# Expert tiles 18 to 24 of a mixture-of-experts stage put into conditional blocks

## The chip, the cores and the metric

The kernel runs on one core of a Trainium2 chip. A core has a matrix engine (TensorE, PE in the profile; its weight loads are shown apart as PEld), a vector engine (VectorE, DVE), a scalar engine (ScalarE, ACT), a general engine (GpSimd, POOL) and a queue engine that issues transfers (SyncE, SP). Each engine takes its own instructions in order and waits on semaphores for the others; 16 DMA engines move data between memory and the on-chip buffers. The metric is the device time of one execution in microseconds (us), as the median of the runs.

## The reference

Sliding-window attention over 8 batches, 8 heads, 576 positions and 64 columns per head is followed by a layer of eight experts over the 4608 resulting tokens of 512 columns. Each token goes to the one expert with the largest router logit:

```
logits = x @ w_gate                       # 4608 x 8
expert_idx = np.argmax(logits, axis=1)
gate_w = probs[np.arange(N), expert_idx]
for e in range(E):                        # 8 experts, rows sorted by expert
    h = np.maximum(x_sorted[lo:hi] @ w1[e], 0.0)     # 512 -> 1024
    y_sorted[lo:hi] = h @ w2[e]                      # 1024 -> 512
return gate_w[:, None] * y_sorted[inv_perm]
```

The inputs come from a fixed seed, so how many tokens each expert gets is the same in every run.

## The kernel before, in words

There are three stages. The first, attention (lines 76 to 282), also computes the router's logits and writes the tokens x to memory (x_dram). The second, routing (lines 285 to 400), gives every token a slot. Slots are grouped in tiles of 256 (TB), and a tile belongs to one expert. Eight experts can leave at most seven extra partly filled tiles, so the kernel provides 4608 / 256 = 18 tiles (NCUT) and 7 more: 25 tiles in all (NTILE), enough for any routing. cum (line 359) holds the running count of tiles that the experts need; its last column is the number of tiles that hold any token. perm_i holds the token of every slot, and a slot without a token points past the end.

The third stage (lines 403 to 470) works through all 25 tiles, one after the other, whether a token lies in them or not. For a tile, fetch reads the tile's expert number from tile_e into a register of SP (line 413), loads w1 and w2 of that expert (2 MB each, lines 415 and 417, from SP) and gathers the 256 token rows in two indirect transfers from POOL (xg, line 421). The rest is the work on the tile: TensorE transposes the rows (tp, line 437), DVE and ACT copy them to the buffer xgT (line 438), TensorE computes hp = w1 x (line 445: 32 instructions, which the profile records as 64 matmuls), DVE and ACT apply the maximum with zero (lines 450 and 452), TensorE computes yp in two halves (line 456: 16 instructions, recorded as 32 matmuls), DVE scales the first half and ACT the second (lines 465 and 463), and POOL scatters each half to the output rows (line 467), leaving out the slots without a token.

w1 and w2 have two buffers each, xg has three of each half, y has four. fetch(i + 1) stands ahead of the work on tile i in the program, and a scheduler then orders the instructions of each engine. Each engine keeps its own order, so SP loads the weights as soon as a buffer is free (w1 of tile i + 2 when hp of tile i is done, w2 of tile i + 2 when yp of tile i is done), and POOL gathers the rows of later tiles between the scatters of earlier ones.

Of the kernel before, what the change touches and what calls it, by code (L numbers as in the profile page):

```python
# [10 lines left out]
F32 = mybir.dt.float32  # L11
I32 = mybir.dt.int32
# [6 lines left out]
WINDOW = 64  # L19
# [3 lines left out]
def _ins(ap: bass.AP, axis: int, n: int) -> bass.AP:  # L23
    """The view of ap that repeats it n times along a new dimension at axis."""
    dims = [list(d) for d in ap.ap]
    dims.insert(axis, [0, n])
    return bass.AP(tensor=ap.tensor, offset=ap.offset, ap=dims)
# [7 lines left out]
def kernel(  # L35
# [10 lines left out]
    nc = tc.nc  # L46
    P = nc.NUM_PARTITIONS
    B, H, S, D = q.shape
    NT, DM = out.shape
    E = moe_w_gate.shape[1]  # L50
    FF = moe_w1.shape[2]
    scale = 1.0 / math.sqrt(D)

    NG = H // 2              # head pairs: one pair fills the 128 partitions
    NB = S // WINDOW         # query blocks of one window; each sees itself and the block before
    GB = 3                   # query blocks handled together
    KB = (S + P - 1) // P    # row tiles of 128, the last one half full
    NV = NB // 2             # whole ones
    SM = NV * P
    BG = 2                   # batches that together fill whole token blocks  # L60
    NTB = BG * S // P        # token blocks in such a group
    NJ = NT // P             # token blocks in all
    FT = FF // P
    TB = 256                 # slots of one expert tile
    C = TB // P
    NTILE = (NT + TB - 1) // TB + E - 1   # enough for any routing
    NS = NTILE * C
    NCUT = (NT + TB - 1) // TB
# [5 lines left out]

    # x in token order, and after it one row of zeros for the slots without a token
    x_dram = dram.tile([NT + 1, DM], F32, name="x_dram")
# [6 lines left out]
    gate_s = consts.tile([P, NS], F32, name="gate_s")  # L83
    tile_e = consts.tile([P, NTILE], I32, name="tile_e")
    zrow = consts.tile([1, DM], F32, name="zrow")
    nc.vector.memset(zrow[:], 0.0)

# [1 line left out]
    with (  # L89
# [11 lines left out]
    ):  # L101
        # additive masks over [(head, query), key]: slot 0 for the first block, whose
        # keys are blocks 0 and 1; the others for the keys of the block before and its own
        mask = att_c.tile([P, 1 + GB, P], F32, name="mask")
        nc.gpsimd.memset(mask[:], 0.0)
        for h in range(2):
# [5 lines left out]
            for m in range(1, 1 + GB):  # L112
# [7 lines left out]
                )  # L120
        # q transposed, each head of the pair in its own columns and zeros beside it
        NQ = 2
# [18 lines left out]
        def load_v(b):  # L141
            va = vp.tile([P, NV, H, D], F32, name="va")
            vb = vp.tile([P, NV, H, D], F32, name="vb")
            for j in range(NV):
                nc.sync.dma_start(out=va[:, j], in_=v[b, :, j * P : (j + 1) * P, :].rearrange("h p d -> p h d"))
            nc.sync.dma_start(out=vb[D:P, NV - 1], in_=v[b, :, SM:S, :].rearrange("h p d -> p h d"))
            # the same keys half a tile later
            nc.gpsimd.tensor_copy(
                out=vb[0:D].rearrange("p j h d -> p (j h d)"), in_=va[D:P].rearrange("p j h d -> p (j h d)")
            )  # L150
            nc.gpsimd.tensor_copy(
                out=vb[D:P, 0 : NV - 1].rearrange("p j h d -> p (j h d)"),
                in_=va[0:D, 1:NV].rearrange("p j h d -> p (j h d)"),
            )
            return va, vb
# [127 lines left out]

# [1 line left out]
    with (  # L285
# [11 lines left out]
        iotas = []  # L297
        e_m = iota([P, E], [[1, E]], base=-E)                    # e - E
        lane = iota([P, P], [[1, P]])
        hi_id = iota([P, NS], [[1, NS]])  # L300
        tile_id = iota([P, NTILE], [[1, NTILE]])
        cuts = iota([P, NCUT], [[TB, NCUT]])
        tok_m = iota([P, NJ], [[P, NJ]], base=-NT, cm=1)         # token - NT, never 0
        before = rt.tile([P, P], F32, name="before")             # [p', p] = p' < p
        ones = rt.tile([P, P], F32, name="ones")
# [4 lines left out]
        )  # L310
        keep = rt.tile([P, E, NJ], F32, name="keep")             # 0 where a scan starts again
        nc.gpsimd.memset(keep[:], 1.0)
        nc.gpsimd.memset(keep[:, :, 0:1], 0.0)

        V = nc.vector
        by_tok = lambda t: t[:].rearrange("p e j -> p j e")
        per_e = lambda t, n: _inner(t[:], n)

        # the first expert of the largest logit, and its probability
        mx = rt.tile([P, NJ], F32, name="r_mx")  # L320
# [14 lines left out]

        # rank of a token among those of its expert: lower partitions of its column, columns before
        ohf = oh[:].rearrange("p e j -> p (e j)")
# [12 lines left out]

        # tiles of each expert, up to and with it, and the slot where it starts
        over = rt.tile([P, E, NCUT], F32, name="over")
# [15 lines left out]
        V.tensor_scalar_min(te[:], te[:], float(E - 1))  # L368
        V.tensor_copy(out=tile_e[:], in_=te[:])

        V.tensor_tensor(out=rank[:], in0=rank[:], in1=per_e(start, NJ), op=ALU.add)
# [11 lines left out]

        # the other way round: token and gate of every slot [slot % P, slot // P]
        lo = rt.tile([P, NJ, P], F32, name="lo")
# [15 lines left out]

# [1 line left out]
    w1v = moe_w1.rearrange("e (g p) f -> p e g f", p=P)  # L403
    w2v = moe_w2.rearrange("e (t p) d -> p e t d", p=P)
    with (
# [21 lines left out]

        fetched = {0: fetch(0)}
        for i in range(NTILE):
            if i + 1 < NTILE:  # L430
                fetched[i + 1] = fetch(i + 1)
            w1, w2, xg = fetched.pop(i)
            xgT = mp.tile([P, NG, TB], F32, name="xgT")
# [19 lines left out]
            for c in range(C):  # L453
                yp = ps_y.tile([P, DM], F32, name="yp")
                for f in range(FT):
                    nc.tensor.matmul(  # L456
                        yp[:], lhsT=hT[:, f, c * P : (c + 1) * P], rhs=w2[:, 0, f, :],
                        start=(f == 0), stop=(f == FT - 1),
                    )
                s = i * C + c  # L460
                y = mp.tile([P, DM], F32, name="y", bufs=4)
                if c % 2:
                    nc.scalar.activation(out=y[:], in_=yp[:], func=AF.Copy, scale=gate_s[:, s : s + 1])  # L463
                else:
                    nc.vector.tensor_scalar_mul(y[:], yp[:], gate_s[:, s : s + 1])  # L465
                # slots without a token point past the end and are left out
                nc.gpsimd.indirect_dma_start(  # L467
                    out=out[:, :], out_offset=bass.IndirectOffsetOnAxis(ap=perm_i[:, s : s + 1], axis=0),
                    in_=y[:], in_offset=None, bounds_check=NT - 1, oob_is_err=False,
                )  # L470


# [26 lines left out]
```

## Time and profile before

| | us |
|---|---|
| median of three runs | 1118.84 |
| lowest and highest run | 1118.69, 1123.08 |
| span of the profiled execution, first to last instruction | 1121.2 |
| TensorE busy in it | 1031.5 (92%) |
| DVE, ACT, POOL busy in it | 350.9, 277.1, 211.8 |

The profile describes one execution; its span is 2.4 us longer than the median of the runs. The attention stage lasts to about 335 us, routing to about 370 us, and the 25 tiles take the rest.

### The profile page before, as it was taken

Reading aid. Unit: us, or ns where it says so; the run is one execution under the profiler, and the core shown is the slowest. Engines: PE = TensorE matmul, PEld = TensorE weight load, DVE = VectorE, ACT = ScalarE, POOL = GpSimd, SP = SyncE. Lnnn points to the kernel's source line nnn. Section 1 sums busy time; section 2 is a strip of 40 time slices with the busy share of each in tenths; the row PEclk is TensorE's granted clock in tenths of the full one; section 3 lists DMA queues with packets and bytes.
Section 4 is the critical chain, followed back from the end, with each engine's and each line's share of the span. In section 5 each row is a group of like instructions: output and inputs, shape, how many; then the busy total and the mean of one; then the engine's idle time right before and its main releaser. Section 6 shows DMA issues by size and latency. Waiting matters only on the chain. (4 is left out here: it accounts for less than half of the span.)

```text
span 1121.2 us, 13320 instructions
## 1 busy us (share of the span) xinstructions
PE 1031.5 (92%) x4868; PEld 753.1 (67%) x4868; DVE 350.9 (31%) x949; ACT 277.1 (25%) x968; POOL 211.8 (19%) x243
## 2 busy tenths in 40 slices
PE   5999898988975699999999999999999999999996
PEld 4888887877864566666666666666666666666663
DVE  5887787877847010111111011111101111111010
ACT  3675675765730000100000000000000000000000
POOL 3442342333220400111111111111111111110000
PEclk9999999999975799999999999999999999999998
DMA  9873654762002774444444555554544445454400
GB/s 198 142 127 109 140 92 133 123 124 89 1 1 85 284 266 176 175 165 170 165 179 178 184 188 187 188 182 170 188 174 170 169 159 174 182 185 150 150 1 0
DMA packets 165491, 166.04 MB, mean 148 GB/s; under 512 B 116912, under 2 KB 116912, under 8 KB 165426
## 3 DMA queue, kind: packets, MB, share of 16 engines
q1 hardware_dynamic: 152242, 133.20, 40.9%
q0 software_dynamic: 8000, 22.56, 5.3%
q10 hardware_dynamic: 5184, 9.44, 2.2%
q8 instruction: 38, 0.62, 0.2%
q14 instruction: 27, 0.22, 0.1%
HBM read 146.29 MB, written 22.55 MB: 151 GB/s over the span
## 5 line engine op out<-in xcount | busy, mean ns | idle before, releaser
L445 PE MATMUL hp<-xgT,w 128*128 128x256 f32 x1600 | 352.3, 381 | 0.8 <-ACT xgT L438 0.8
L456 PE MATMUL yp<-w,hT 128*128 128x512 f32 x800 | 347.4, 592 | 0.0
L445 PEld LDWEIGHTS hp<-xgT,w 128*128 128x128 f32 x1600 | 303.1, 191 | 43.3 <-ACT xgT L438 1.0
L456 PEld LDWEIGHTS yp<-w,hT 128*128 128x128 f32 x800 | 152.0, 190 | 180.7 <-issue 179.4
L467 POOL DMA_INDIRECT out_dram<-y,perm_i x50 | 50.0, 1001 | 532.9 <-DVE y L465 492.1
L452 DVE TENSOR_SCALAR hT<-hp 128x256 f32<-128x256 f32 x100 | 42.5, 425 | 302.6 <-PE hp L445 302.6
L450 ACT ACTIVATE hT<-hp 128x256 f32<-128x256 f32 x100 | 38.4, 384 | 326.3 <-PE hp L445 245.3
L204 POOL TENSOR_TENSOR pr<-pr,sm 128x384 f32<-128x384 f32 x96 | 79.4, 828 | 206.2 <-DVE sm L203 68.9
L198 ACT ACTIVATE pr<-pr,mx 128x128 f32<-128x128 f32 x288 | 112.6, 392 | 21.5 <-DVE mx L195 18.7
L463 ACT ACTIVATE y<-yp,gate_s 128x512 f32<-128x512 f32 x25 | 17.2, 688 | 334.4 <-PE yp L456 334.4
L186 PE MATMUL sc<-kT,qd 128*128 128x128 f32 x576 | 90.5, 287 | 2.5 <-DVE pr L192 1.3
L465 DVE TENSOR_SCALAR y<-yp,gate_s 128x512 f32<-128x512 f32 x25 | 18.8, 751 | 202.2 <-PE yp L456 202.2
L186 PEld LDWEIGHTS sc<-kT,qd 128*128 128x128 f32 x576 | 75.8, 196 | 7.0 <-DVE pr L192 3.9
L421 POOL DMA_INDIRECT xg<-x_dram,perm_i x50 | 49.3, 986 | 157.2 <-PE tp L437 100.2
L210 PE MATMUL pt<-ident,pr 128*128 128x128 f32 x288 | 54.5, 292 | 19.1 <-POOL pr L204 17.5
L438 DVE COPY xgT<-tp 128x512 f32<-128x512 f32 x25 | 17.3, 692 | 150.7 <-PE tp L437 149.3
L217 PE MATMUL pv<-pT,va 128*128 128x128 f32 x320 | 61.4, 291 | 3.0 <-DVE pT L212 2.7
L192 DVE TENSOR_TENSOR pr<-sc,mask 128x384 f32<-128x384 f32 x96 | 52.7, 549 | 17.0 <-PE sc L186 14.8
L212 DVE COPY pT<-pt 128x384 f32<-128x384 f32 x96 | 52.6, 550 | 17.1 <-PE pt L210 16.2
L210 PEld LDWEIGHTS pt<-ident,pr 128*128 128x128 f32 x288 | 33.7, 147 | 30.4 <-POOL pr L204 29.4
L198 ACT ACTIVATION_READ_ACCUMULATOR pr<-pr,mx 128x1 f32 x288 | 53.9, 187 | 0.0
L217 PE MATMUL pv<-pT,vb 128*128 128x128 f32 x256 | 52.3, 288 | 0.6 <-ACT xT L224 0.3
(94 smaller groups left out, 760.7 us busy)
## 6 DMA issues: line engine op xcount, KB each, us to landing
w<-in_moe_w_dram SPq DMA_DIRECT2D x50, 2048.0 KB, 9.4
x_dram<-xs ACTq DMA_DIRECT2D x36, 256.0 KB, 2.0
qs<-in_q_dram SPq DMA_DIRECT2D x32, 256.0 KB, 5.0
ks<-in_k_dram SPq DMA_DIRECT2D x32, 256.0 KB, 5.1
va<-in_v_dram SPq DMA_DIRECT2D x32, 256.0 KB, 5.0
qs<-in_q_dram SPq DMA_DIRECT2D x8, 128.0 KB, 5.0
ks<-in_k_dram SPq DMA_DIRECT2D x8, 128.0 KB, 4.6
vb<-in_v_dram SPq DMA_DIRECT2D x8, 128.0 KB, 4.5
```

What stands on the lines that cost most here:

```text
L186: nc.tensor.matmul(sc[:, n, :], lhsT=qd[:, i].rearrange("d h s -> d (h s)"), rhs=kT[:, k0 : k0 + P], start=True, stop=True,)
L192: nc.vector.tensor_tensor(out=pr[:], in0=sc[:], in1=mask[:, m0 : m0 + GB, :], op=ALU.add)
L198: nc.scalar.activation(out=pr[:, n, :], in_=pr[:, n, :], func=AF.Exp, scale=scale, bias=mx[:, n : n + 1], accum_out=sm[:, n : n + 1],)
L204: nc.gpsimd.tensor_tensor(out=pr[:], in0=pr[:], in1=_inner(sm[:], P), op=ALU.mult)
L210: nc.tensor.transpose(out=pt[:, n, :], in_=pr[:, n, :], identity=ident[:])
L212: nc.vector.tensor_copy(out=pT[:], in_=pt[:])
L217: nc.tensor.matmul(pv[:, n, :], lhsT=vt[:, 2 * g : 2 * g + 2, :].rearrange("p h d -> p (h d)"), rhs=pT[:, n, :], start=True, stop=True,)
L421: nc.gpsimd.indirect_dma_start(out=t[:], out_offset=None, in_=x_dram[:, :], in_offset=bass.IndirectOffsetOnAxis(ap=perm_i[:, i * C + c : i ...
L445: nc.tensor.matmul(hp[:], lhsT=w1[:, 0, g, f * P : (f + 1) * P], rhs=xgT[:, g, :], start=(g == 0), stop=(g == NG - 1),)
L452: nc.vector.tensor_scalar_max(hT[:, f, :], hp[:], 0.0)
L456: nc.tensor.matmul(yp[:], lhsT=hT[:, f, c * P : (c + 1) * P], rhs=w2[:, 0, f, :], start=(f == 0), stop=(f == FT - 1),)
L467: nc.gpsimd.indirect_dma_start(out=out[:, :], out_offset=bass.IndirectOffsetOnAxis(ap=perm_i[:, s : s + 1], axis=0), in_=y[:], in_offset=N ...
```

## The change

Three things are changed; the deletion of comments, which the diff also holds, is left out below. The work on a tile becomes a function, tile_work. The first 18 tiles are done by it as before, with the fetch of the next tile ahead of the work, except that the fetch of tile 18 is no longer among these. For tiles 18 to 24 the number of used tiles is read from a new buffer, used_i, into a register of each engine, and each tile stands in a block of its own that is entered only when used > i; the fetch of the tile stands in the block too.

```
 tile_e = consts.tile([P, NTILE], I32, name="tile_e")
+used_i = consts.tile([P, 1], I32, name="used_i")
...
 V.tensor_copy(out=tile_e[:], in_=te[:])
+V.tensor_copy(out=used_i[:], in_=cum[:, E - 1 : E])
...
-        fetched = {0: fetch(0)}
-        for i in range(NTILE):
-            if i + 1 < NTILE:
-                fetched[i + 1] = fetch(i + 1)
-            w1, w2, xg = fetched.pop(i)
+        def tile_work(i, w1, w2, xg):
             xgT = mp.tile([P, NG, TB], F32, name="xgT")
...
+        fetched = {0: fetch(0)}
+        for i in range(NCUT):
+            if i + 1 < NCUT:
+                fetched[i + 1] = fetch(i + 1)
+            tile_work(i, *fetched.pop(i))
+        used = nc.values_load(used_i[0:1, 0:1], min_val=NCUT, max_val=NTILE)
+        for i in range(NCUT, NTILE):
+            with tc.If(used > i):
+                tile_work(i, *fetch(i))
```

No wait between all engines is put ahead of a block or behind it: each engine reads used for itself, compares and branches at its own time. In place of a skipped block an engine runs a few semaphore instructions, which bring the counts to where the block would have left them.

On POOL, around the gathers of tile 18, the kernel before has this order (xg0_6095 and xg1_6097 are the two halves of tile 18's rows; y_5863 is the second half of tile 15, y_5956 the first half of tile 16):

```order
L421 DMA xg0_5988<-x_dram_60,perm_i_68 128x512
L467 DMA out_0_dram<-y_5756,perm_i_68 4608x512
L421 DMA xg1_5990<-x_dram_60,perm_i_68 128x512
L467 DMA out_0_dram<-y_5849,perm_i_68 4608x512
L421 DMA xg0_6095<-x_dram_60,perm_i_68 128x512
L467 DMA out_0_dram<-y_5863,perm_i_68 4608x512
L421 DMA xg1_6097<-x_dram_60,perm_i_68 128x512
L467 DMA out_0_dram<-y_5956,perm_i_68 4608x512
```

And the changed kernel has this (xg0_6202 and xg1_6204 are tile 18's rows, xg0_6310 and xg1_6312 tile 19's; y_6155 and y_6169 are tile 17, y_6277 and y_6291 tile 18):

```order
L465 DMA out_0_dram<-y_6155,perm_i_68 4608x512
L465 DMA out_0_dram<-y_6169,perm_i_68 4608x512
L475 TENSOR_LOAD used_i_71
L477 COMPARE_AND_BRANCH
L423 DMA xg0_6202<-x_dram_60,perm_i_68 128x512
L423 DMA xg1_6204<-x_dram_60,perm_i_68 128x512
L465 DMA out_0_dram<-y_6277,perm_i_68 4608x512
L465 DMA out_0_dram<-y_6291,perm_i_68 4608x512
L477 UNCONDITIONAL_BRANCH
L477 ISA
L477 UNCONDITIONAL_BRANCH
L477 COMPARE_AND_BRANCH
```

The gathers of tile 18 have moved from beside the scatters of tile 15 to behind both scatters of tile 17, and those of tile 19 stand behind both scatters of tile 18.

On PE the kernel before has this order at the same place (xg_6095 and xg_6097 are tile 18, xg_6202 and xg_6204 tile 19, w_5984 to w_6093 the weights of tiles 17 and 18):

```order
L437 MATMUL tp<-ident,xg_6095 128x128 x3
L445 MATMUL hp<-xgT,w_5984 128x256 x32
L456 MATMUL yp<-w_5986,hT 128x512 x16
L437 MATMUL tp<-ident,xg_6095 128x128
L437 MATMUL tp<-ident,xg_6097 128x128 x4
L437 MATMUL tp<-ident,xg_6202 128x128 x3
L445 MATMUL hp<-xgT,w_6091 128x256 x32
L456 MATMUL yp<-w_6093,hT 128x512 x16
```

And the changed kernel has this (w_5986 and w_5988 belong to tile 17, w_6198 and w_6200 to tile 18):

```order
L443 MATMUL hp<-xgT,w_5986 128x256 x32
L454 MATMUL yp<-w_5988,hT 128x512 x16
L475 TENSOR_LOAD used_i
L477 COMPARE_AND_BRANCH
L435 MATMUL tp<-ident,xg_6202 128x128 x4
L435 MATMUL tp<-ident,xg_6204 128x128 x4
L443 MATMUL hp<-xgT,w_6198 128x256 x32
L454 MATMUL yp<-w_6200,hT 128x512 x16
L477 UNCONDITIONAL_BRANCH x2
```

The transposes of a tile were begun ahead of the hp of the tile before; now all eight stand behind the branch, directly ahead of their own hp.

On SP the changed kernel has this order from tile 19 on (w1_6306 and w2_6308 are the weights of tile 19, w1_6414 and w2_6416 those of tile 20):

```order
L417 DMA w1_6306<-in_moe_w1_dram 128x4x1024
L419 ISA
L419 DMA w2_6308<-in_moe_w2_dram 128x8x512
L477 UNCONDITIONAL_BRANCH x2
L477 COMPARE_AND_BRANCH
L415 TENSOR_LOAD tile_e_70
L415 ISA x2
L417 ISA
L417 DMA w1_6414<-in_moe_w1_dram 128x4x1024
L419 ISA
L419 DMA w2_6416<-in_moe_w2_dram 128x8x512
```

The weight loads keep their order and what they wait for, which is the matmuls that free a buffer; what moved is the reading of tile_e, which now stands inside each block.

## Rows read from the trace of the kernel before

**Rows 1.** The page: busy time of the engines; PE and granted clock in 40 slices.

```profile
PE 1031.5 (92%) x4868; PEld 753.1 (67%) x4868; DVE 350.9 (31%) x949; ACT 277.1 (25%) x968; POOL 211.8 (19%) x243
PE   5999898988975699999999999999999999999996
PEclk9999999999975799999999999999999999999998
```

**Rows 2.** Two stretches: length, busy per engine (instructions), granted clock, DMA share, GB/s.

```profile
core 0: us, PE busy (x) PEld busy (x) DVE busy (x) ACT busy (x) POOL busy (x), PEclk, DMA share, GB/s
430.00:1010.00 580.00, 572.46 (x2074) 380.65 (x2073) 62.15 (x119) 53.65 (x119) 77.74 (x78) 1.00 0.50 177
1110.00:1121.20 11.20, 0.09 (x1) 0.00 (x0) 0.00 (x0) 0.69 (x1) 0.98 (x1) 0.71 0.00 0
```

**Rows 3.** Timeline of PE, tiles 22 to 24: start, us, instructions, idle before.

```profile
1024.07 14.05 PE L445 MATMUL hp<-xgT,w 128*128 128x256 f32 x64
...
1051.69 0.71 PE L437 MATMUL tp<-ident,xg 128*128 128x128 f32 x5
...
1053.19 14.05 PE L445 MATMUL hp<-xgT,w 128*128 128x256 f32 x64
...
1067.08 13.90 PE L456 MATMUL yp<-w,hT 128*128 128x512 f32 x32
...
1082.28 14.08 PE L445 MATMUL hp<-xgT,w 128*128 128x256 f32 x64 [0.76 <-ACT xgT L438]
```

**Rows 4.** Scatters of tiles 0 to 20, then of tiles 21 to 24.

```profile
L467 POOL DMA_INDIRECT out_dram<-y,perm_i x42: 985/1003/1028, 408.4 to 995.3; - x42
...
DMA to landing us min/median/max: 2.6/4.6/8.2
...
L467 POOL DMA_INDIRECT out_dram<-y,perm_i x8: 985/985/1010, 1016.9 to 1111.1; - x8
...
DMA to landing us min/median/max: 2.1/2.1/6.2
```

**Rows 5.** Gathers from 430 to 1010 us; below them POOL's timeline, one gather and scatter.

```profile
L421 POOL DMA_INDIRECT xg<-x_dram,perm_i x38: 986/992/995, 470.0 to 996.6; - x38
...
DMA to landing us min/median/max: 6.4/7.3/8.6
...
500.30 1.00 POOL L467 DMA_INDIRECT out_dram<-y,perm_i  x1 [0.30 <-issue]
501.61 0.99 POOL L421 DMA_INDIRECT xg<-x_dram,perm_i  x1 [0.30 <-issue]
```

**Rows 6.** The last w2 load, on SP, and its time to landing.

```profile
L417 SPq DMA_DIRECT2D w<-in_moe_w_dram x1: 373/373/373, 1051.9 to 1051.9; - x1
...
DMA to landing us min/median/max: 8.5/8.5/8.5
```

**Rows 7.** Second scatters of tiles 22, 23 with landing; timeline, end of tile 24.

```profile
1052.91 0.98 POOL L467 DMA_INDIRECT out_dram<-y,perm_i  x1 [5.86 <-ACT y L463]
DMA to landing us min/median/max: 6.2/6.2/6.2
...
1082.03 0.98 POOL L467 DMA_INDIRECT out_dram<-y,perm_i  x1 [5.86 <-ACT y L463]
DMA to landing us min/median/max: 2.1/2.1/2.1
...
1096.20 13.90 PE L456 MATMUL yp<-w,hT 128*128 128x512 f32 x32
...
1110.18 0.69 ACT L463 ACTIVATE y<-yp,gate_s 128x512 f32<-128x512 f32 x1 [13.40 <-PE yp L456]
1111.14 0.98 POOL L467 DMA_INDIRECT out_dram<-y,perm_i  x1 [5.86 <-ACT y L463]
```

**Rows 8.** SP's queue: reading an expert number into a register (ns min/median/max).

```profile
L413 SPq TENSOR_LOAD <-tile_e x25: 261/267/757, 345.2 to 361.0; - x25
```

**Rows 9.** Single microseconds: PE busy, granted clock, DMA share, GB/s.

```profile
369.00:370.00 1.00, 0.66 (x6) 1.00 0.00 0
373.00:374.00 1.00, 0.00 (x0) 1.00 0.96 385
374.00:375.00 1.00, 0.00 (x0) 0.50 1.01 414
386.00:387.00 1.00, 1.00 (x4) 0.50 1.03 389
388.00:389.00 1.00, 1.00 (x6) 1.00 1.02 381
1114.00:1115.00 1.00, 0.00 (x0) 0.85 0.00 0
```

**Rows 10.** Timeline of the first tiles: copy, transposes and hp behind the first gathers.

```profile
380.55 0.59 ACT L438 COPY xgT<-tp 128x512 f32<-128x512 f32 x1 [26.12 <-PE tp L437]
...
384.39 1.09 PE L437 MATMUL tp<-ident,xg 128*128 128x128 f32 x4 [0.58 <-DMA xg<-x_dram,perm_i]
385.27 15.16 PE L445 MATMUL hp<-xgT,w 128*128 128x256 f32 x64
```

**Rows 11.** POOL's queue behind the last scatter (ns min/median/max; starts).

```profile
L494 POOLq EVENT_SEMAPHORE  x4: 17/17/17, 1120.4 to 1121.1; - x4
L494 POOLq DRAIN  x3: 40/107/9462, 1110.9 to 1120.9; - x3
```

**Rows 12.** The page, part 3: a DMA queue that brings instructions (packets, MB, share).

```profile
q8 instruction: 38, 0.62, 0.2%
```

## The prediction, made before the changed kernel ran

> **What bounds the kernel now.** I read the page first, then two stretches, then the timeline of PE, and last the transfers. From 370 us on PE is busy in nearly every slice and holds the full clock [rows 1]; in the stretch from 430 to 1010 us it is busy for 572.46 of 580 us, while DVE, ACT and POOL are each under 14% and the DMA engines at half [rows 2]. The tiles are bound by PE alone, and a tile lasts 29.12 us: hp starts at 1024.07 and at 1053.19, again 29.09 us later for the last one [rows 3]. Of that, 13.90 us is yp, and from the end of a yp to the next hp 1.30 us pass (1067.08 + 13.90 = 1080.98 to 1082.28) [rows 3]. Such a row is worth 29.1 us for every tile that PE needn't do, and a stall on PE costs its full length.
>
> **How many tiles go.** The landing times of the scatters tell which tiles hold tokens. None of the 42 scatters of tiles 0 to 20 lands in under 2.6 us; of the eight of tiles 21 to 24 the shortest and the median are 2.1 us [rows 4], which no filled half reaches. Two of the eight take 6.2 us; one is the second half of tile 22, issued 1.0 us after the last w2 load, the same half of tile 23 with no load beside it takes 2.1 [rows 6, 7]. So a load in flight adds 4.1 us, and tiles 21 to 24 write nothing. The reference's router on its fixed inputs agrees: 669, 400, 748, 505, 592, 390, 566 and 738 tokens need 3+2+3+2+3+2+3+3 = 21 tiles. Tiles 18, 19 and 20 are entered, 21 to 24 skipped. Removed: 4 x 29.12 = 116.5 us, all of it PE's path.
>
> **What an entered block costs.** What moves is the gather. Before, POOL issues it some two tiles ahead, and it is never waited for in the steady stretch. Now POOL's order puts it behind both scatters of the tile before, so it can't start until that tile is through PE, and PE has nothing else to do. Queued behind it on POOL are only the tile's own scatters; who waits is PE, with DVE and ACT behind. I count from the end of the last yp, 1110.10 us in the trace (1096.20 + 13.90) [rows 7].
>
> - ACT scales the second half, POOL issues the scatter from 1111.14 to 1112.12: 2.02 us after the yp [rows 7].
> - Between two issues on POOL lie 0.30 us [rows 5]. Tile 18 adds the reading of used, 0.27 us on SP [rows 8]. A branch has no row: its bounds are zero and, if it has to fetch its instructions, one shortest landing, 2.1 us [rows 4]; I take zero, since an entered block follows directly behind its branch in the program, and keep the other end for the range. The first gather starts at 2.6, the second 1.3 us later (0.99 + 0.30) at 3.9.
> - A gather lands 7.3 us after its issue in the middle, 6.4 to 8.6 [rows 5]. Those were issued just as the w2 load two tiles on had started. That is the same here: SP isn't held by the blocks, and the w2 of tile 19 is issued when the yp of tile 17 ends, the w2 of tile 20 when that of tile 18 ends. So 7.3 holds for tiles 18 and 19: landings at 9.9 and 11.2. For tile 20 no load is left, since tile 21 isn't entered; the nearest rows are 2.1 to 2.8 us for lone scatters [rows 4] or 7.3 less the 4.1 of the load. I take 3.0, nearer to those: 5.3 and 6.6 (gathers at 2.3 and 3.6).
> - [...] Four transposes take 1.09 us then, the copy by ACT 0.59 [rows 10]; with 0.2 for two handovers hp of tiles 18 and 19 starts at 11.2 + 1.09 + 0.59 + 0.2 = 13.1, of tile 20 at 8.5. Less the 1.30 that stood there before: 11.8, 11.8 and 7.2.
> - An hp that begins at 0.50 took 15.16 us in place of 14.05 [rows 3, 10], since the clock was back within its first 3 us [rows 9]: 1.1 more for each.
>
> So tiles 18 and 19 cost 12.9 each and tile 20 costs 8.3: 34.1 us. The weights cost nothing: w1 of tile 18 waits for the hp of tile 16 as before and w2 for its yp, a tile and more ahead; were that cover gone, an entered tile would wait 8.5 us and more for w2 [rows 6].
>
> **The rest.** Computing used_i is one cast on DVE in the routing stage, 0.2 us as a generous estimate. At the end each engine passes four skipped blocks. On POOL each is a wait, a few semaphore instructions of 17 ns [rows 11] and branches without a row; SP and POOL then wait for the last scatter as now. The span's end is set by a drain on POOL that starts at 1110.9 and lasts 9.46 us [rows 11], behind which up to some 7 us of PE's way through its skipped blocks can hide. I take 1.5 us, from 0 to 8 (four fetches at 2.1).
>
> [...]
>
> **Sum.** -116.5 + 34.1 + 0.2 + 1.5 = -80.7 us. The profiled span of 1121.2 becomes 1040.5; taken from the median of the runs, which is 2.4 us shorter than that span, it is 1118.84 - 80.7 = 1038 us.
>
> **The rivals.** (1) *A lighter entry.* The gathers of tiles 18 and 19 land like a lone transfer, because they are issued some 2 us later behind the load than before, and the clock doesn't fall. Each then costs some 6 to 7 us: 3 x 6.5 = 20, so 1024 us. Against it: the scatter of tile 22, 1.0 us behind the load, still took 6.2 [rows 7]. (2) *Branches that wait for instructions.* [...] If each jump waits at least one shortest landing of 2.1 us, and POOL's entries too, three entries and four exits cost 15 us: 1052 us; with the cover of the drain at the end half of that. For it: nothing in the trace before ever jumped. Against it: POOL's blocks are short, and PE's entries lie under the wait for the gather. [...] (3) *POOL's branch waits like its drain.* If reading used or branching on POOL must let the last indirect transfer finish as the drain does, each entry costs up to 8.3 us more (1112.12 to 1120.4 [rows 7, 11]): 1062 us. I see no reason that it should; a gather follows a scatter after 0.30 us [rows 5]. (4) *Slower: all seven blocks are entered.* The place is the comparison with used. An entered block costs 12.9 us and a skipped one gives 29.12, so it decides from five entered blocks on (5 x 12.9 = 64.5 against 58.2); with seven it is 1118.84 + 7 x 12.9 = 1209 us, and the change would not do what it says. The landings of 2.1 us [rows 4] speak against it.
>
> **How the numbers follow.** Forecast 0.66, rival 1 0.12, rival 2 0.14, rival 3 0.06, rival 4 0.02. About 0.5% is what a measurement of this kernel can tell from no change; every case but the last is faster by far more than that: faster 0.97, same 0.01, slower 0.02. The range goes from between the forecast and rival 1 (all three gathers short but the clock lost, about 1027) to rival 2 with its upper end (1055); rivals 3 and 4 and the far half of rival 1 stay outside.
>
> **What would show it.** Right: PE's records of hp and yp fall from 1600 and 800 to 1344 and 672; three stretches near the end in which PE idles for about 10, 10 and 5 us with the gather as the releaser, granted clock 0.50 behind each; w1 and w2 of tiles 18 to 20 landed long before. The end of the last yp lies some 82 us earlier than 1110.1, and the tail behind it is 11 to 13 us. Wrong: idle times on PE that end with a weight load, gathers that start later than 3 us after the yp, a tail of 15 us and more, or no fall of the clock.

## The result, and the profile after

The changed kernel takes 1050.8 us (median; 1046.79 to 1053.1), beside 1120.96 us for the kernel before on the same chip: a ratio of 0.937, with a 95% interval from 0.934 to 0.940. (A ratio here and below is to the kernel before as it was run beside that version; the medians of the runs come from several chips, where the kernel before took 1119.5 to 1122.8 us. Medians are over all executions and ratios over the fast ones, which parts them in run 2 alone, where one of four executions took 5084.58 us for a reason that is not on record.) The forecast of 1038 us named the right case and the right order of the terms, and the time lies inside the range, 12.8 us above the point. Two terms were too small: the end of the kernel, by 8 us, and the slow start of PE in an entered block, by 3.5 us.

The profiled execution has a span of 1048.1 us, in place of 1121.2. First the page: busy time of PE, its share in 40 slices, the granted clock in the same slices, and PE's two large groups (count, busy us, mean ns, idle time before and its releaser).

```profile
PE 922.8 (88%) x4452; PEld 678.0 (65%) x4452; DVE 337.9 (32%) x926; ACT 266.6 (25%) x944; POOL 195.3 (19%) x227
...
PE   5899898898887569999999999999999999695792
...
PEclk9999999999996679999999999999999999897986
...
L443 PE MATMUL hp<-xgT,w 128*128 128x256 f32 x1344 | 302.9, 387 | 2.9 <-ACT xgT L436 2.9
L454 PE MATMUL yp<-w,hT 128*128 128x512 f32 x672 | 291.8, 592 | 0.0
```

The records of hp and yp fell to 1344 and 672, which is 21 tiles: four tiles are skipped, as the landings of their scatters had told [rows 4]. PE's busy time fell by 1031.5 - 922.8 = 108.7 us [rows 1]. The last slices are new: before, PE was full up to the last one; now there are three dips, to 6, 5 and 7 tenths, with a clock of 7 to 9 tenths in those slices, and a last slice with a 2, in which PE has long finished.

The dips are the three entered blocks. The timeline of PE from tile 17 on (start us, us, instructions; in brackets the idle time before and what ended it):

```profile
889.51 13.90 PE L454 MATMUL yp<-w,hT 128*128 128x512 f32 x32
912.61 1.09 PE L435 MATMUL tp<-ident,xg 128*128 128x128 f32 x4 [9.21 <-DMA xg<-x_dram,perm_i]
913.85 1.09 PE L435 MATMUL tp<-ident,xg 128*128 128x128 f32 x4 [0.16 <-DMA xg<-x_dram,perm_i]
915.66 16.55 PE L443 MATMUL hp<-xgT,w 128*128 128x256 f32 x64 [0.72 <-ACT xgT L436]
932.05 13.90 PE L454 MATMUL yp<-w,hT 128*128 128x512 f32 x32
955.97 1.98 PE L435 MATMUL tp<-ident,xg 128*128 128x128 f32 x8 [10.03 <-DMA xg<-x_dram,perm_i]
958.67 15.54 PE L443 MATMUL hp<-xgT,w 128*128 128x256 f32 x64 [0.72 <-ACT xgT L436]
974.05 13.90 PE L454 MATMUL yp<-w,hT 128*128 128x512 f32 x32
993.82 1.09 PE L435 MATMUL tp<-ident,xg 128*128 128x128 f32 x4 [5.87 <-DMA xg<-x_dram,perm_i]
...
996.93 16.88 PE L443 MATMUL hp<-xgT,w 128*128 128x256 f32 x64 [0.72 <-ACT xgT L436]
1013.64 13.90 PE L454 MATMUL yp<-w,hT 128*128 128x512 f32 x32
```

From one yp to the next pass 42.54, 42.00 and 39.59 us, where 29.12 stood before [rows 3]: the entries cost 13.4, 12.9 and 10.5 us, 36.8 in all. The gather is the releaser each time. Its time to landing at tile 18 and at tile 20 (a line's instructions in a stretch; ns min/median/max, first and last start):

```profile
L423 POOL DMA_INDIRECT xg<-x_dram,perm_i x2: 967/980/993, 905.7 to 907.0; - x2
...
DMA to landing us min/median/max: 6.7/6.7/6.7
...
L423 POOL DMA_INDIRECT xg<-x_dram,perm_i x2: 961/978/994, 990.3 to 991.6; - x2
...
DMA to landing us min/median/max: 3.4/3.4/3.4
```

The clock during tile 18's entry, in stretches (start and end us, length, PE's busy time, granted clock, DMA share, GB/s):

```profile
core 0: us, PE busy (x), PEclk, DMA share, GB/s
904.00:912.00 8.00, 0.00 (x0) 0.69 0.90 303
912.00:916.00 4.00, 2.51 (x9) 0.50 0.13 49
916.00:921.00 5.00, 5.00 (x13) 0.53 0.00 0
921.00:932.00 11.00, 11.00 (x52) 1.00 0.00 0
```

In the first 5 us of hp the granted clock is 0.53 on average and PE gets through 13 matmuls; the 11 us at 1.00 behind them hold 52.

And the end. The last scatter; the instructions that belong to the line of the condition, L477, on PE and POOL; and the drain at the end of the program:

```profile
1028.59 1.01 POOL L465 DMA_INDIRECT out_dram<-y,perm_i  x1 [5.83 <-ACTq L477]
...
L477 PEldq COMPARE_BRANCH  x10: 73/177/3127, 896.1 to 1031.7; - x10
...
L477 POOLq COMPARE_BRANCH  x10: 34/40/50, 904.8 to 1038.2; - x10
...
L477 POOLq INC_SWDGE_SEM  x4: 1844/1844/1863, 1031.6 to 1038.5; - x4
...
L502 POOLq DRAIN  x3: 46/107/6922, 1040.4 to 1047.9; - x3
```

The last yp ends at 1027.54 us and the span at 1048.1: a tail of 20.6 us, where 11.1 stood before [rows 2, 7]. In it POOL issues the last scatter, which lands 2.9 us after its start at 1028.59, then makes four increments of 1.84 us, one for each skipped block, from 1031.6 to 1040.4, and only then starts a drain of 6.92 us.

The account on the two spans: -116.5 for four tiles, +36.8 for three entries, +9.5 for the tail, and -2.9 because the whole row of tiles began earlier (the first gather at 367.92 us, before at 370.88). Together -73.1, from 1121.2 to 1048.1. The 2.9 us are not put down to the change: in ten profiles of this study the first gather lies anywhere from 367.9 to 372.0 us, though the program ahead of it is the same but for the cast to used_i.

### The profile page after: what moved, and what is told of

The parts are those of the page before. It is cut to its first block, busy times and chain, and to the rows that moved or that the text cites. A ratio compares the mean times of both kernels' runs of the same rounds, so it can differ in the third digit from the quotient of the medians.

```text
span 1048.1 us, 12418 instructions
## 1 busy us (share of the span) xinstructions
PE 922.8 (88%) x4452; PEld 678.0 (65%) x4452; DVE 337.9 (32%) x926; ACT 266.6 (25%) x944; POOL 195.3 (19%) x227
## 5 line engine op out<-in xcount | busy, mean ns | idle before, releaser
L443 PE MATMUL hp<-xgT,w 128*128 128x256 f32 x1344 | 302.9, 387 | 2.9 <-ACT xgT L436 2.9
L454 PE MATMUL yp<-w,hT 128*128 128x512 f32 x672 | 291.8, 592 | 0.0
L443 PEld LDWEIGHTS hp<-xgT,w 128*128 128x128 f32 x1344 | 259.6, 194 | 41.9 <-ACT xgT L436 4.4
L454 PEld LDWEIGHTS yp<-w,hT 128*128 128x128 f32 x672 | 127.7, 190 | 151.8 <-issue 150.7
L465 POOL DMA_INDIRECT out_dram<-y,perm_i x42 | 41.9, 998 | 506.2 <-DVE y L463 420.9
L450 DVE TENSOR_SCALAR hT<-hp 128x256 f32<-128x256 f32 x84 | 35.7, 425 | 265.3 <-PE hp L443 265.3
L448 ACT ACTIVATE hT<-hp 128x256 f32<-128x256 f32 x84 | 32.3, 384 | 281.0 <-PE hp L443 227.0
L211 PE MATMUL pt<-ident,pr 128*128 128x128 f32 x288 | 53.6, 287 | 20.6 <-POOL pr L205 18.9
L435 PE MATMUL tp<-ident,xg 128*128 128x128 f32 x168 | 31.4, 322 | 40.4 <-DMA xg<-x_dram,perm_i 26.4
L436 DVE COPY xgT<-tp 128x512 f32<-128x512 f32 x21 | 14.5, 692 | 153.6 <-PE tp L435 142.8
L423 POOL DMA_INDIRECT xg<-x_dram,perm_i x42 | 41.1, 979 | 119.0 <-PE tp L435 64.2
L435 PEld LDWEIGHTS tp<-ident,xg 128*128 128x128 f32 x168 | 22.4, 162 | 56.9 <-issue 46.2
```

Source lines behind the costliest of these rows:

```text
L211: nc.tensor.transpose(out=pt[:, n, :], in_=pr[:, n, :], identity=ident[:])
L423: nc.gpsimd.indirect_dma_start(out=t[:], out_offset=None, in_=x_dram[:, :], in_offset=bass.IndirectOffsetOnAxis(ap=perm_i[:, i * C + c : i ...
L435: nc.tensor.transpose(out=tp[:, g, :], in_=xg[c][:, g * P : (g + 1) * P], identity=ident[:])
L443: nc.tensor.matmul(hp[:], lhsT=w1[:, 0, g, f * P : (f + 1) * P], rhs=xgT[:, g, :], start=(g == 0), stop=(g == NG - 1),)
L454: nc.tensor.matmul(yp[:], lhsT=hT[:, f, c * P : (c + 1) * P], rhs=w2[:, 0, f, :], start=(f == 0), stop=(f == FT - 1),)
L465: nc.gpsimd.indirect_dma_start(out=out[:, :], out_offset=bass.IndirectOffsetOnAxis(ap=perm_i[:, s : s + 1], axis=0), in_=y[:], in_offset=N ...
```

## The experiments

My theory after the result: an entered block costs the wait for its gather and the clock lost in it; a skipped block costs nothing on PE, but one increment on POOL, at the end of the program. Rivals: weights or instructions that come late, reading or branching itself, and a drain that would have lasted as long anyway.

**1. No blocks, 21 tiles.** The loop of the unconditional tiles runs to 21 and the blocks go. (It leaves out what the blocks are for: other inputs could need more tiles.)

```
-        for i in range(NCUT):
-            if i + 1 < NCUT:
+        for i in range(21):
+            if i + 1 < 21:
...
-        used = nc.values_load(used_i[0:1, 0:1], min_val=NCUT, max_val=NTILE)
-        for i in range(NCUT, NTILE):
-            with tc.If(used > i):
-                tile_work(i, *fetch(i))
```

> Tiles 0 to 20 straight through with the fetch one tile ahead, no block and no branch; tiles 21 to 24 are left out, which is right only for these inputs. It is the removal alone. My account of the changed kernel: four tiles give 4 x 29.12 = 116.5 us, three entered blocks take back 36.8 us, the four skipped ones 9.5. Then this is 1121 - 116.5 = 1004.5 us (1000 to 1009). If instead a removed tile is worth less than its period (the end of the kernel, or the start of the tiles, taking something back whatever stands there), it is 1015 us or more.

Measured: 1004.61 us, ratio 0.895 (0.892 to 0.898), span 1005.2. Its tail behind the last yp is 9.8 us (995.39 to 1005.2). So all that the conditions cost together, entries and tail, is about 46 us. Beside the kernel before on the same chip (1122.75 us) it is 118.1 us faster; of that the four tiles at the price of [rows 3] are 116.5, and a tail that is 1.3 us shorter is most of the rest.

**2. Three blocks in place of seven.** Only tiles 18 to 20 have blocks; all are entered, none is skipped. (Tiles 21 to 24 are left out.)

```
-        for i in range(NCUT, NTILE):
+        for i in range(NCUT, 21):
             with tc.If(used > i):
```

> The changed kernel without its four skipped blocks: tiles 18, 19 and 20 in blocks as they are, tiles 21 to 24 left out of the program, which is right only for these inputs. If the four increments of 1.84 us on POOL in the skipped blocks (one in 2.23 us) make the longer end, the end behind the last yp falls from 20.6 to 11 or 12 us and the time from 1051 to 1042 us (1038 to 1045). If the longer end comes from PE's jump of 3.1 us, from the drain on POOL or from a last scatter that moves rows, it stays at 1050 us.

Measured: 1041.58 us, ratio 0.928 (0.924 to 0.932). The last yp on PE and the drain on POOL:

```profile
1014.92 13.90 PE L454 MATMUL yp<-w,hT 128*128 128x512 f32 x32
...
L502 POOLq DRAIN  x3: 40/113/8032, 1029.8 to 1038.4; - x3
```

The last yp ends at 1028.82 and the span at 1038.6: the tail is 9.8 us, as without blocks. The entries stay as they were. The skipped blocks make the long tail.

**3. Gathers ahead of the blocks.** POOL gathers the rows of tiles 18 to 24 unconditionally, into buffers of their own; the scheduler puts these 14 gathers into the first tile's time.

```
...
+            if i == NCUT - 2:
+                for j in range(NCUT, NTILE):
+                    rows[j] = gather(j, ahead=True)
             tile_work(i, *fetched.pop(i))
...
             with tc.If(used > i):
-                tile_work(i, *fetch(i))
+                tile_work(i, *weights(i), rows[i])
```

> The changed kernel with one thing moved: the gathers of tiles 18 to 24 are issued ahead of the blocks, into buffers of their own, and only the weights' loads and the work stay inside. If the gather is the whole price of an entered block, PE waits 1 to 3 us at each entry in place of 12.3, 12.7 and 9.0, its clock does not fall, and the time is 1051 - 34 = 1017 us (1011 to 1023), with the skipped blocks still there. If branching, reading used or the weights inside the block hold PE too, an entry still costs 5 us or more and the time is 1028 us or more.

Measured: 1013.41 us, ratio 0.9035 (0.9003 to 0.9068). The timeline of PE at tile 18:

```profile
889.84 13.90 PE L460 MATMUL yp<-w,hT 128*128 128x512 f32 x32
903.57 1.04 PE L441 MATMUL tp<-ident,xa 128*128 128x128 f32 x8
905.33 14.08 PE L449 MATMUL hp<-xgT,w 128*128 128x256 f32 x64 [0.72 <-ACT xgT L442]
```

A yp follows the one before after 29.41 us; an entry costs 0.3 us in place of 12.3. So the reading of used, the branches and the weights, which are all still there, cost next to nothing, and the gather with the clock is the whole price. What is left against run 1 is the tail: 18.8 us, with four increments. (The price is that all 14 gathers run, those of the skipped tiles too, each into a buffer of its own.)

**4. All seven blocks entered.** used is set to 25, whatever the routing.

```
-        V.tensor_copy(out=used_i[:], in_=cum[:, E - 1 : E])
+        V.tensor_scalar_max(used_i[:], cum[:, E - 1 : E], float(NTILE))
```

> The changed kernel with used_i forced to 25, so that all seven blocks are entered and none is skipped. If an entry costs 13.1 us with the weights of a later tile being loaded beside its gather, and 10.5 without, six of the first kind and one of the second and an end as before give 1121 + 6 x 13.1 + 10.5 = 1210 us (1203 to 1217): the block design loses 8% where the tiles are full. If the price belongs to the first entries (code that is fetched, the first reading of used), the later ones cost less and it is below 1190 us.

Measured: 1210.91 us, ratio 1.080 (1.077 to 1.083). The slower rival with its price of 12.9 us a block had said 1209; from one yp to the next pass 39.9 to 43.0 us seven times. Nothing is skipped, and the tail is 11.1 us (1196.29 to 1207.4), as before the change. With all seven blocks entered the change costs 8%; an input that needs all 25 tiles was not run.

**5. Blocks inside one another.** Since a tile can only be in use if the one ahead of it is, block 19 may lie inside block 18, and so on; used = 21 then leads to one skip.

```
-        for i in range(NCUT, NTILE):
-            with tc.If(used > i):
+        with ExitStack() as blocks:
+            for i in range(NCUT, NTILE):
+                blocks.enter_context(tc.If(used > i))
                 tile_work(i, *fetch(i))
```

> The seven blocks lie inside one another, so that used = 21 leads to one skip in place of four; entries as in the change. Theory: the tail of 20.6 us behind the last yp is long because POOL increments its transfer semaphores once per skipped block (4 x 1.84 us, 2.2 us from start to start) before it can begin the drain of about 7 us. With one skip three of these go: 20.6 - 3 x 2.2 = 14.0 us, about 1044 us, PE as in the change. Rival: the time of an increment goes with how much it makes up for; one skip of four tiles then takes as long as four skips, and the time stays at 1051. Second rival: the drain waits for something else that ends at a fixed distance from the last scatter; also 1051.

Measured: 1043.31 us, ratio 0.9324 (0.9298 to 0.9349). POOL's increments and its drain at the end:

```profile
L476 POOLq INC_SWDGE_SEM  x1: 1868/1868/1868, 1030.6 to 1030.6; - x1
...
L503 POOLq DRAIN  x3: 46/107/6924, 1032.7 to 1040.2; - x3
```

One increment makes up for four tiles and takes 1.87 us, as one for a single tile does. The tail is 13.7 us (1026.66 to 1040.4), 6.9 less. The drain takes 6.92 us again and has only moved with the increment: it isn't something that ends at a fixed distance from the last scatter. Both rivals fall.

**6. Weights two tiles earlier.** Four buffers each for w1 and w2, so that no 2 MB load starts with the gathers of tiles 18 and 19.

```
-            w1 = wp.tile([P, 1, NG, FF], F32, name="w1")
+            w1 = wp.tile([P, 1, NG, FF], F32, name="w1", bufs=4)
...
-            w2 = wp.tile([P, 1, FT, DM], F32, name="w2")
+            w2 = wp.tile([P, 1, FT, DM], F32, name="w2", bufs=4)
```

> Four buffers for w1 and w2 in place of two: the weights of tiles 19 and 20 are loaded up to two tiles earlier, and no 2 MB load starts together with the gathers of tiles 18 to 20. Theory: a gather lands in 6.7 to 7.5 us when a weight load is in flight and in 3.4 when none is, as it did at tile 20. Then PE's idle time at tiles 18 and 19 falls from 9.2 to 10.0 us to about 6, as at tile 20, and the kernel gains 2 x 3.5 = 7 us: 1044. Rival: the gather of tile 20 was short for another reason (its place as the last one), and tiles 18 and 19 stay as they were: 1051.

Measured: 1045.75 us, ratio 0.9333 (0.9308 to 0.9358), an interval that still overlaps that of the change; the trace is clearer. The gathers of tile 18, and PE's wait for the first of them:

```profile
L423 POOL DMA_INDIRECT xg<-x_dram,perm_i x2: 967/982/997, 909.8 to 911.1; - x2
...
DMA to landing us min/median/max: 3.5/3.5/3.5
```

```profile
913.27 1.09 PE L435 MATMUL tp<-ident,xg 128*128 128x128 f32 x4 [5.83 <-DMA xg<-x_dram,perm_i]
```

All six gathers land in 3.4 to 3.6 us, and the three waits are 5.83, 5.94 and 5.95 us. The entries cost 10.5, 9.5 and 10.6 us, 30.6 in place of 36.8. The load beside it is what made tiles 18 and 19 dearer than tile 20. The other 6 us of a wait are the scatter ahead and the gather itself; hp stays long all the same, 16.76, 15.68 and 16.92 us.

**7 and 8. Work for PE in the wait.** PE transposes the identity into the tile's own PSUM buffer until the gather lands: at first (run 7) 64, 64 and 40 times, then (run 8) 84, 84 and 50 times, with 4 more ahead of the second gather's transposes. The edit of run 8:

```
                 tp = ps_xt.tile([P, NG, P], F32, name="tp")
+                for g in range(warm if c == 0 else min(warm, 4)):
+                    nc.tensor.transpose(out=tp[:, g % NG, :], in_=ident[:], identity=ident[:])
...
-                tile_work(i, *fetch(i))
+                tile_work(i, *fetch(i), warm=50 if i == 20 else 84)
```

> In each block PE runs transposes of the identity (64 at tiles 18 and 19, 40 at tile 20) into the same PSUM tile while it waits for the gather; nothing else changes, the gather's wait stays. Theory: the granted clock falls to 0.50 in the idle time and costs each entry 0.55 us in its last four transposes and 1.5 to 2.8 us in hp. With PE busy the clock stays at 1.00 until shortly before the gather lands, hp is back at 14.05 us: -(2.5 + 1.5 + 2.8) - 3 x 0.55 = -8.4 us, about 1042. Rival: the clock falls anyway, or hp is longer in an entered block for another reason (instructions, weights that come late): 1051, with hp at 15.5 us and more.

Measured: 1050.41 us, ratio 0.937 (0.9347 to 0.9392): no gain. By itself this looks like the rival. But the wait wasn't filled. The timeline of PE at tile 18, and the clock in two stretches:

```profile
906.95 7.15 PE L435 MATMUL tp<-ident 128*128 128x128 f32 x64
916.03 0.66 PE L437 MATMUL tp<-ident,xg 128*128 128x128 f32 x4 [1.93 <-DMA xg<-x_dram,perm_i]
...
919.17 16.55 PE L445 MATMUL hp<-xgT,w 128*128 128x256 f32 x64 [0.72 <-ACT xgT L438]
```

```profile
916.00:919.00 3.00, 1.74 (x8) 0.73 0.08 27
919.00:924.00 5.00, 4.83 (x11) 0.50 0.00 0
```

The clock was still 1.00 when the gather landed and fell at 917.4 us (a mean of 0.73 over the three microseconds from 916 means full clock for the first 1.4; the expectation below has 917.7), after a pause of 1.93 us and one of 0.68, and it was away for hp's first 5 us. So the run could not tell the two apart, and a second one filled more of the wait.

> As the run with transposes of the identity in the wait, but enough of them to fill it: 84, 84 and 50 ahead of the first gather's transposes, and 4 ahead of the second's. With 64, 64 and 40 PE still stood idle for 1.93, 2.72 and 1.44 us before the first gather landed and 0.5 to 0.7 us before the second, and the granted clock fell to 0.50 at 917.7 us and came back within 925, in the middle of hp, which took 16.55, 15.77 and 15.57 us. Theory: what lengthens hp is the lost clock alone; with the wait filled the clock stays at 1.00 and hp takes 14.05 us, so that the three entries cost some 36.8 - 6.8 - 1.7 = 28 us and the time is about 1042. Rival: hp is long in an entered block for another reason as well; hp stays over 15 us with the clock at 1.00, and the time over 1046.

Measured: 1039.74 us, ratio 0.9284 (0.9264 to 0.9304). Timeline and clock at tile 18:

```profile
900.36 9.33 PE L435 MATMUL tp<-ident 128*128 128x128 f32 x84
909.53 0.60 PE L437 MATMUL tp<-ident,xg 128*128 128x128 f32 x4
...
911.94 14.08 PE L445 MATMUL hp<-xgT,w 128*128 128x256 f32 x64 [0.72 <-ACT xgT L438]
```

```profile
900.00:912.00 12.00, 11.28 (x99) 1.00 0.68 219
912.00:926.00 14.00, 14.00 (x65) 1.00 0.00 1
```

hp takes 14.08 us in all three blocks, at a clock of 1.00. The wait is filled to the end at tile 18 alone. At tile 19 PE still stood idle for 1.85 us, and the clock stayed at 1.00:

```profile
950.77 0.66 PE L437 MATMUL tp<-ident,xg 128*128 128x128 f32 x4 [1.85 <-DMA xg<-x_dram,perm_i]
```

The entries cost 10.1, 12.0 and 7.1 us, 29.3 in all: with the clock kept, 7.5 of the 36.8 us go. The wait for the gather stays; at tile 19 it even ended about 1 us later behind the yp than in the change (11.0 us, from 939.76 to 950.77, in place of 10.0).

**9 and 10. Both cures at once.** Gathers ahead, and blocks inside one another.

> Gathers of tiles 18 to 24 issued ahead of the blocks and the blocks inside one another: both terms at once. The run with the gathers ahead alone took 1013.4 us, with a tail of 18.8 us behind the last yp, four increments of 2.0 us among it. Theory: one increment in place of four takes some 3 x 2.3 = 7 us off: 1006, next to the 1004.6 of the version with 21 tiles and no blocks. Rival: the increment grows with what it makes up for: 1013.

Measured: 1021.32 us, ratio 0.9127 (0.9102 to 0.9153), slower than run 3 by 8 us. The tail did as expected (14.5 us, 1003.95 to 1018.5), but the row of tiles ended 12 us later. The place is the first tile: an ACT row, a row on the waits of DVE (us in total, times, longest) and a PE row.

```profile
403.01 0.38 ACT L454 ACTIVATE hT<-hp 128x256 f32<-128x256 f32 x1 [15.30 <-remote]
```

```profile
DVE hT L456 <- remote: 13.7, 1, 13.7
```

```profile
403.45 6.35 PE L449 MATMUL hp<-xgT,w 128*128 128x256 f32 x16 [9.25 <-issue]
```

ACT and DVE didn't empty the buffers of hp, of which there are three, and PE ran out of them. Both were waiting: "remote" means that the semaphore's event belongs to no instruction's recorded end. In run 3 the releaser of the same ACT rows is PE's hp, and the second follows the first after 3.45 us (387.57, 391.02). Here the first starts at 387.33 us and the second at 403.01, where 390.8 would have been its time; PE's records of hp run on to 394.20. So it seems to be PE's signal, or the end of PE's work, that came some 12 us late, and not ACT that was slow. From 376 to 402 us the DMA engines were full (a share of 0.98 to 1.05 in every two microseconds) with the 14 gathers and the first weights. In run 3 they moved the same 9.37 MB from 380 to 406 us, and ACT wasn't held. So I moved the gathers: their indices come from a copy that can only be made when a y buffer of tile 12 is free.

```
-                    in_offset=bass.IndirectOffsetOnAxis(ap=perm_i[:, i * C + c : i * C + c + 1], axis=0),
+                    in_offset=bass.IndirectOffsetOnAxis(
+                        ap=perm_late[:, (i - NCUT) * C + c : (i - NCUT) * C + c + 1] if ahead
+                        else perm_i[:, i * C + c : i * C + c + 1], axis=0),
...
-            if i == NCUT - 2:
+            if i == NCUT - 4:
+                late = mp.tile([P, DM], F32, name="y", bufs=4)
+                V.tensor_copy(out=late[:, 0 : (NTILE - NCUT) * C], in_=perm_i[:, NCUT * C : NTILE * C])
+                V.tensor_copy(out=perm_late[:], in_=late[:, 0 : (NTILE - NCUT) * C])
                 for j in range(NCUT, NTILE):
```

> Gathers of tiles 18 to 24 ahead of the blocks, and blocks inside one another, as in the run that took 1021.3 us; but the 14 gathers take their indices from a copy that is made when tile 14 begins, so that they are issued around tile 14 and not during the first tile. In that run ACT stood still for 15.3 us and with it PE for 9.25 us in the first tile's hp, while the DMA engines were full with these gathers and the first weights. Theory: the full DMA engines held something that ACT needed; with the gathers later the stall goes and the time is 1021.3 - 12 = 1009, below the 1013.4 of the gathers ahead alone. Rival: the stall belongs to this program wherever the gathers lie, or the burst stalls tile 14 to 16 instead: 1015 to 1021.

Measured: 1007.65 us, ratio 0.9001 (0.8977 to 0.9025); this is the lowest time of a version that still serves every routing, though its interval overlaps that of run 3 (0.9003 to 0.9068); the version without conditions had a ratio of 0.895. POOL's increment and drain at its end:

```profile
L492 POOLq INC_SWDGE_SEM  x1: 2028/2028/2028, 995.3 to 995.3; - x1
...
L519 POOLq DRAIN  x3: 46/107/7577, 997.5 to 1005.7; - x3
```

The stall is gone, no tile around the burst of gathers is longer than 29.12 us, and the entries are 0.3 us each. What held PE's signal to ACT and DVE in run 9 is not shown: that the stall goes when the gathers move speaks for the full DMA engines, that run 3 didn't have it says that they alone don't suffice. It stays open.

## Why the prediction was right or wrong

**Four tiles go: right.** 1344 and 672 records, and run 1 gives the worth of the tiles without the blocks.

**The gather is the price of an entry: right, and so nearly was its size.** The gathers start 2.3 and 3.6 us behind the yp (905.74 and 907.04, after 903.41), land after 6.7 to 7.5 us at tiles 18 and 19, where 7.3 was taken, and after 3.4 at tile 20, where 3.0 was taken. From yp to hp pass 12.25, 12.72 and 8.98 us; forecast were 13.1, 13.1 and 8.5. That the difference between the tiles is the weight load was inferred from scatters [rows 4, 7]; run 6 shows it for gathers. The weights themselves were never waited for.

**hp at half clock: the right mechanism, half its size.** At tile 18 PE stopped at 903.41 us, and the granted clock was 1.00 up to 907, 0.53 on average in the microsecond from there and 0.50 behind it. The slow hp was priced at 1.1 us by the first tile's hp, where the clock came back within 3 us [rows 9, 10]. Here it came back after 5.0, 3.0 and 5.7 us, and hp took 2.5, 1.5 and 2.8 us more, 6.8 in place of 3.3. One example was taken for a constant. Run 8 shows that it is the clock and nothing else (14.08 us at 1.00).

**The tail: the step that failed.** The forecast took 1.5 us; it was 9.5. The prediction counted a skipped block on POOL as "a wait, a few semaphore instructions of 17 ns [rows 11] and branches without a row" and let the drain of 9.46 us cover the rest. Neither held. At a skip POOL has an increment, INC_SWDGE_SEM (four in the change, one in run 5, none on the line of the condition in runs 2 and 4), and it takes 1.84 us, a hundred times the 17 ns; four take 8.8 us with what lies between them. Why it takes so long isn't shown. The trace of the kernel before even has an instruction of this name, at the start of the program, and by that row it would have been cheap too:

```profile
L485 POOLq INC_SWDGE_SEM  x1: 31/31/31, 0.2 to 0.2; - x1
```

And the drain covers next to nothing that stands ahead of it on the same queue: it ends 6.9 us after the last increment here, 6.9 us after the last scatter was issued in runs 1 and 2, and 8.2 us after that in the kernel before (1112.12 to 1120.37 [rows 7, 11]). So the wait for the scatter to land (2.0 us, from 1029.6 to 1031.6) and the 8.8 us of increments come on top, less the 1.3 us by which the drain is shorter: 9.5. The bound of 8 us that stood beside the 1.5 was meant for four fetches of instructions, not for this, and 9.5 lies outside it. That the time fell inside the range, because rival 2 had stretched it to 1055, is luck.

**Rival 2, branches that wait for instructions.** Seven jumps at 2.1 us each were an estimate of mine. The profile has one long branch: of PE's ten one takes 3.13 us, the others mostly some 0.1 to 0.2 us. In runs 3, 5, 6, 8 and 10, which skip too, PE's longest takes 3.21 to 4.62 us; in runs 2 and 4, where nothing is skipped, it takes 0.18 us. The queue of [rows 12] began one packet of 16 KB at 1028.9 us, 0.5 us into the long branch; that the branch waited for it wasn't tested by a run. It costs nothing, since PE's last branch begins at 1031.7 and POOL's work ends with the span at 1048.1. The time came close to this rival's 1052 by another way, and only the trace tells the two apart. The branches on the other engines take 34 to 63 ns, the ten of an engine about half a microsecond together.

**Rivals 1, 3 and 4.** Rival 1 (gathers that land like a lone transfer, no loss of clock) didn't come; runs 6 and 8 show what each half of it needs and gives, 6.2 and 7.5 us. Rival 3 falls: a gather follows the scatter after 0.30 us, as before [rows 5]; the reading of used (once, 0.51 us from 904.2) and the branch (34 to 50 ns) stand in between and lie under the issue of that scatter. Rival 4's price was right, as run 4 shows; its condition wasn't met.

**The signs named beforehand.** The three stretches "in which PE idles for about 10, 10 and 5 us" came as 9.2, 10.0 and 5.9. "A tail of 15 us and more" stood among the signs of an error, and that is what came.

**The distance of 12.8 us.** The tail makes 8.0 of it and the entries 2.7 (36.8 less 34.1). The earlier start of the tiles takes off 2.9, and the 0.2 that was set down for computing used, a cast of 0.15 us, doesn't show. The rest, 5.1 us, lies between spans and medians: the median of before was 2.4 us under its profiled span, that of after is 2.7 us above its own.

## What to carry to other kernels

In this kernel a conditional block costs twice: entered, it begins with a gather that can't be issued early (5.9 to 10.0 us of idle PE), and with a clock of 0.50 behind the wait (1.5 to 2.8 us in hp); skipped, it leaves an increment of 1.84 us on POOL, the queue that sets the end. Put the inputs' transfers ahead of the condition (12.3 us an entry became 0.3) and, as runs 9 and 10 suggest, not into a stretch in which the DMA engines are full; and nest conditions that imply one another, so that one skip stands for many (1.87 us for four tiles in run 5). Price the skipped way instruction by instruction, too; a row of a cheap semaphore instruction says nothing of another one, nor of the same one in another place (0.03 us at the start, 1.84 here).

## What the runs showed of the hardware that I had not expected

- POOL's increment at a skip takes 1.84 to 2.04 us, for one skipped tile as for four; the one at the start takes 0.03 us, in the kernel before and in the changed one.
- POOL's drain at the end takes 6.9 to 7.6 us behind increments, 6.9 us of it even where every transfer has landed 9 us before; right behind a scatter, and counted from before its issue, it takes 8.0 to 9.5 us. With the gathers ahead both are the longer ones (increments of 1.98 to 2.04 us in runs 3 and 10, a drain of 7.6 us in runs 3, 9 and 10); why isn't shown.
- The clock fell to 0.50 in run 7 though PE had worked for 7.15 of the 9.1 us ahead of the first gather's landing (906.95 to 916.03). In run 8 it stayed at 1.00, at tile 18 with the wait filled and at tile 19 with 1.85 us of it left open; what makes the difference to run 7 there isn't shown.
- A gather of 128 rows in an entered block landed in 3.4 to 3.6 us with no load beside it (tile 20 of the change, all six of run 6) and in 6.7 to 7.5 beside a 2 MB load (tiles 18 and 19 of the change).
